# One quadrant fold per four attention slots, values five slots behind, K loaded further ahead, in a grouped-query attention block on one core

## The chip, the core and the metric

The kernel runs on one NeuronCore of a Trainium2 chip. Its engines work side by side and wait for each other through semaphores: TensorE (PE; matmuls, into PSUM), its weight loads (PEld), VectorE (DVE), ScalarE (ACT), GpSimd (POOL), and SyncE (SP), which here issues nearly all DMA transfers. The metric is the device time of one execution in microseconds (us), lower is better; single executions of one kernel lie 0.4 us apart in the three of the kernel before.

A profile is one execution. Its first 23 us (loads, first projections) vary. So besides the times this document uses a length read from the start times in the trace: **from the first scores matmul to the last matmul of all** (start to start). It is called the *stretch*; it is 321.51 us in the kernel before.

## The reference

Two independent problems, A and B, of the same form; outputs side by side.

```python
B, Sq, D = 16, 32, 1024;  Hq, Hkv, Sk, Dh = 32, 4, 512, 128
q = (x @ wq).reshape(B, Sq, Hq, Dh).transpose(0, 2, 1, 3)
k, v = repeat(k_cache, 8, axis=1), repeat(v_cache, 8, axis=1)
p = softmax(einsum("bhqd,bhkd->bhqk", q, k) * Dh ** -0.5)
out = einsum("bhqk,bhkd->bhqd", p, v).transpose(0, 2, 1, 3).reshape(B, Sq, Hq * Dh) @ wo
```

All bf16. One (batch, kv head) pair has 8 query heads x 32 queries = 256 columns against 512 keys. There are 2 x 64 = 128 such pairs.

## The kernel before

The kernel goes through 128 *slots*, one pair each, plus a few to drain. In slot i it issues the scores of pair i (keys on partitions), their exp without a row maximum, the row sums on VectorE, and the values product of an earlier pair. Around these it weaves *units*: single matmuls of the query and output projections, so that PE always has work. K and V come in *groups* of four slots, 512 KB each; K is transposed by the DMA. A *fold* is a small PE matmul: it adds the row sums, which VectorE leaves in four partition quadrants, over the quadrants. In the code and the profile s_ps are scores, p_sb their exps, cs the row sums before the fold, kT and v_sb groups of K and V, wo_sb 1 MB blocks of the output weights.

```python
def partial_sums(i):                       # DVE: 32x32 block transpose + sum -> per quadrant
    j, q = divmod(i, 2)
    if q == 0: parts[j] = work.tile([P, 2, KC, REP], FP32, name="parts")
    nc.vector.tensor_reduce(out=parts[j][:, q, :, :]..., in_=st[i]["p"]..., axis=AX.X,
                            op=ALU.add, apply_transpose=True)
def chunk_sums(j): ...                     # DVE: sum over the 4 key chunks -> cs
def fold_sums(j):                          # PE: adds the 4 partition quadrants, spreads the result
    sums = pair[j] = psum.tile([P, 2 * REP], FP32, name="sums", tag="sums", bufs=1)
    nc.tensor.matmul(sums[:], lhsT=fold[:]..., rhs=cs[:]..., start=True, stop=True)
def reciprocals(j):                        # DVE: 1/sum, then spread over the queries
    nc.vector.reciprocal(out=rall[:, j, :], in_=pair.pop(j)[:])
    r = rcp[j] = work.tile([P, 2 * REP, SQ], FP32, name="r")
    nc.vector.transpose(...)

# [...] plan of loads: the sync engine gets them in the order of their slots
for j in range(2, 2 * NG // GRP):          # GRP = 4, NG = 64
    at(GRP * (j - 1), load_k, j)
    at(GRP * (j - 1) + 2, load_v, j)
# [...]
        at(NG - 12 + nh * 8 + hg * 2, load_wo, 0, nh, hg)   # output weights of A, 8 x 1 MB

for i in range(total_slots + 3):
    live = i < total_slots
    j, odd = divmod(i, 2)
    if live: do_loads(i); scores(i)        # 4 matmuls of 256 columns
    run(units, 1)                          # 1 matmul of 512 columns
    if not odd and 1 <= j <= NG: chunk_sums(j - 1)
    if i >= 3: values(i - 3)               # 4 matmuls of 256 columns
    if odd and 1 <= j <= NG: reciprocals(j - 1)
    if not odd and j >= 2: normalize(j - 2)
    run(units, 5)
    if not odd and 1 <= j <= NG: fold_sums(j - 1)
    if live: partial_sums(i)
    run(units, 1 - (i % 4 == 3))
```

## Time and profile before

350.65 us, median of three runs (350.25 to 350.69). The busy times of the profiled execution (engine, busy us, share of the span):

```profile
span 349.1 us, 5460 instructions
PE 340.7 (98%) x2163; PEld 221.0 (63%) x2204; DVE 283.4 (81%) x421; ACT 179.6 (51%) x196; POOL 8.9 (3%) x21
PE 94%; DMA 3%; issue 1%; DVE 1%; ACT 0%; SPq 0%
```

The last line is the chain that ended last, by engine: PE bounds the kernel. A busy share of 98% alone would not say how full PE is, because matmuls overlap. The start times do. Consecutive 512-column matmuls start 216 ns apart and 256-column ones 109 ns apart. This is the warm spacing N/2.4 + 2.5 ns that the Trainium skill gives ("TensorE: Matmul & The Clock Gate", section "Back-to-back issue gap"), and the trace agrees. So each slot can be checked: take the time from its scores to the next slot's, and subtract its matmuls at that spacing. What is left is its *gap*:

| slots of the kernel before | gap each | sum in the stretch |
|---|---|---|
| without a fold | 0.00 us | 0.0 us |
| with a fold (63 in the loop) | 0.042 to 0.044 us | 2.71 us |
| extra in slots 80 and 118 | 0.33 and 0.12 us | 0.45 us |

These are the groups of instructions that the change touches (line, engine, operation, output<-input, shapes, count | busy us, mean ns of one | idle time of the engine before it, and the releaser):

```profile
L390 DVE TRANSPOSE_TENSOR_REDUCE parts<-p_sb 128x32 f32<-128x1024 bf16 x128 | 158.2, 1236 | 21.5 <-ACT p_sb L379 20.9
L407 PE MATMUL sums<-cs,fold 128*128 128x16 f32 x64 | 22.9, 357 | 0.1
L399 DVE TENSOR_REDUCE cs<-parts 128x16 fp32r<-128x64 f32 x64 | 16.9, 264 | 2.2
L407 PEld LDWEIGHTS sums<-cs,fold 128*128 128x128 f32 x64 | 12.1, 190 | 8.3 <-DVE cs L399 0.9
L416 DVE RECIPROCAL rall<-sums 128x16 f32<-128x16 f32 x64 | 14.1, 220 | 0.0
```

The fold's row says 357 ns. That is its time from start to end, most of it behind the matmul ahead of it. What it takes from PE is the 43 ns gap. One such slot in the timeline of PE (start us, length us):

```profile
154.43 1.24 PE L312 MATMUL q_ps<-xT,wq_sb 128*128 128x512 bf16 x5
155.32 0.36 PE L407 MATMUL sums<-cs,fold 128*128 128x16 f32 x1
155.54 0.39 PE L312 MATMUL q_ps<-xT,wq_sb 128*128 128x512 bf16 x1
155.77 0.60 PE L371 MATMUL s_ps<-qT,kT 128*128 128x256 bf16 x4
```

The fifth projection matmul of the first line starts at 155.29 and the next one, across the fold, at 155.54: 0.25 us instead of 0.216.

The sync engine's queue around the change from problem A to B, where loads are densest (start us, time the issue took us):

```profile
152.75 9.52 SPq L288 DMA_TRANSPOSE kT<-in_B_k_cache_dram  x1
162.31 0.58 SPq L267 DMA_DIRECT2D wo_sb<-in_A_wo_dram  x1
162.99 0.53 SPq L294 DMA_DIRECT2D v_sb<-in_B_v_cache_dram  x1
163.61 0.45 SPq L267 DMA_DIRECT2D wo_sb<-in_A_wo_dram  x1
164.16 8.96 SPq L288 DMA_TRANSPOSE kT<-in_B_k_cache_dram  x1
```

One group's worth of loads (K, V, two output-weight blocks) takes 11.4 us from K to K in these lines (10.9 us on average from the V load shown to the second one after it), one group of slots on PE 9.4 us. The V load in these lines is that of group 16, the first of problem B. It is issued at 163.0, landed at 170.4, and is first used at 180.0: 9.7 us to spare.

### The profile page before, as it was taken

The page shows a single profiled execution, that of the slowest core. Times are in us where ns is not written, and L with a number is a line of the kernel's source. Part 1 is how long each engine was busy: PE and PEld are TensorE (multiplying, and loading weights), DVE is VectorE, ACT ScalarE, POOL GpSimd, SP SyncE. Part 2 cuts the span into 40 slices and gives each one's busy share as a digit, 9 for nine tenths or more (in the row PEclk, how much of TensorE's full clock was granted, in tenths as well). Part 3 has the DMA queues.
Part 4 walks back from the last instruction along what each step waited for, and adds up shares of the span by engine and source line. Part 5 has one row for each costly group of instructions (what it writes and reads, how often), then busy time and mean ns, then how long its engine had stood idle before and what let it go on. Part 6 is the DMA issues. An engine that isn't in the chain of part 4 may idle for free.

```text
span 349.1 us, 5460 instructions
## 1 busy us (share of the span) xinstructions
PE 340.7 (98%) x2163; PEld 221.0 (63%) x2204; DVE 283.4 (81%) x421; ACT 179.6 (51%) x196; POOL 8.9 (3%) x21
## 2 busy tenths in 40 slices
PE   8999999999999999999999999999999999999995
PEld 4556666666666666666666666666666666666554
DVE  2218888988988898898889999999989999899710
ACT  2247667666666666666654454454454445445000
POOL 0000000000000000000000000000000000000010
PEclk9999999999999999999999999999999999999999
DMA  7999999999996999999999659996579975400000
GB/s 242 275 251 339 181 274 264 254 269 249 270 214 176 199 233 233 296 275 210 305 313 192 175 126 289 348 199 122 135 258 287 284 182 97 116 17 0 15 32 20
DMA packets 125085, 71.70 MB, mean 205 GB/s; under 512 B 73632, under 2 KB 124064, under 8 KB 125056
## 3 DMA queue, kind: packets, MB, share of 16 engines
q1 hardware_dynamic: 122848, 68.24, 81.1%
q0 software_dynamic: 720, 1.97, 1.6%
q10 hardware_dynamic: 1488, 1.11, 1.1%
q8 instruction: 18, 0.29, 0.4%
q14 instruction: 11, 0.09, 0.1%
HBM read 51.38 MB, written 2.10 MB: 153 GB/s over the span
## 4 chain that ended last, share of the span: by engine, by line
PE 94%; DMA 3%; issue 1%; DVE 1%; ACT 0%; SPq 0%
PE f_ps L331 31%; PE q_ps L312 30%; PE ob L431 16%; PE s_ps L371 16%; DMA wq_sb<-in_A_wq_dram 2%; DMA x_sb<-in_A_x_dram 1%; DVE parts L390 0%; PE sums L407 0%; DVE o_sb L343 0%; ACT o_sb L341 0%; DVE cs L399 0%; PE ok_ps L614 0%; SPq L651 0%
## 5 line engine op out<-in xcount | busy, mean ns | idle before, releaser
L379 ACT ACTIVATE p_sb<-s_ps,shift 128x1024 bf16<-128x1024 f32 x128 | 142.5, 1114 | 113.1 <-PE s_ps L371 100.4
L390 DVE TRANSPOSE_TENSOR_REDUCE parts<-p_sb 128x32 f32<-128x1024 bf16 x128 | 158.2, 1236 | 21.5 <-ACT p_sb L379 20.9
L331 PE MATMUL f_ps<-wo_sb,oT 128*128 128x512 bf16 (+1 forms) x524 | 127.9, 367 | 0.4
L312 PE MATMUL q_ps<-xT,wq_sb 128*128 128x512 bf16 x475 | 124.8, 380 | 0.6
L371 PE MATMUL s_ps<-qT,kT 128*128 128x256 bf16 x512 | 76.8, 273 | 0.9
L431 PE MATMUL ob<-p_sb,v_sb 128*128 128x256 bf16 x512 | 76.8, 273 | 0.6
L331 PEld LDWEIGHTS <-oT 128*128 128x128 bf16 x544 | 53.0, 98 | 33.8
L312 PEld LDWEIGHTS <-wq_sb 128*128 128x128 bf16 x496 | 48.3, 98 | 35.1 <-DMA wq_sb<-in_A_wq_dram 0.6
L371 PEld LDWEIGHTS <-kT 128*128 128x128 bf16 x512 | 56.9, 113 | 20.9
L431 PEld LDWEIGHTS <-v_sb 128*128 128x128 bf16 x512 | 50.1, 98 | 19.8 <-DVE oT L453 0.3
L453 DVE TENSOR_TENSOR oT<-r,ob 128x512 bf16<-128x512 f32 x64 | 43.9, 685 | 12.7 <-PE ob L431 9.3
L320 ACT CAST qT<-q_ps 128x512 bf16<-128x512 f32 x62 | 36.1, 583 | 23.7 <-PE q_ps L312 20.8
L418 DVE STREAM_TRANSPOSE r<-rall 128x512 f32<-128x512 f32 x64 | 45.5, 711 | 2.2
L407 PE MATMUL sums<-cs,fold 128*128 128x16 f32 x64 | 22.9, 357 | 0.1
L343 DVE CAST o_sb<-f_ps 128x512 bf16<-128x512 f32 (+1 forms) x16 | 10.8, 673 | 10.8 <-PE f_ps L331 10.0
L399 DVE TENSOR_REDUCE cs<-parts 128x16 fp32r<-128x64 f32 x64 | 16.9, 264 | 2.2
L407 PEld LDWEIGHTS sums<-cs,fold 128*128 128x128 f32 x64 | 12.1, 190 | 8.3 <-DVE cs L399 0.9
L345 POOL DMA_DIRECT2D out_dram<-o_sb x15 | 8.2, 549 | 329.7 <-DVE o_sb L343 299.0
L416 DVE RECIPROCAL rall<-sums 128x16 f32<-128x16 f32 x64 | 14.1, 220 | 0.0
L341 ACT CAST o_sb<-f_ps 128x256 bf16<-128x256 f32 x1 | 0.4, 372 | 22.1 <-PE f_ps L331 22.1
L497 DVE COPY xT<-xT_ps 128x512 bf16<-128x512 bf16 x4 | 1.7, 424 | 5.3 <-PE xT_ps L493 5.3
L484 PE MATMUL warm_ps<-warm 128*128 128x512 bf16 x10 | 4.2, 580 | 1.3 <-DVE warm L230 1.3
(26 smaller groups left out, 22.8 us busy)
## 6 DMA issues: line engine op xcount, KB each, us to landing
v_sb<-in_A_v_cache_dram SPq DMA_DIRECT2D x16, 512.0 KB, 4.9
wq_sb<-in_B_wq_dram SPq DMA_DIRECT2D x8, 1024.0 KB, 6.5
wo_sb<-in_A_wo_dram SPq DMA_DIRECT2D x8, 1024.0 KB, 7.6
v_sb<-in_B_v_cache_dram SPq DMA_DIRECT2D x16, 512.0 KB, 4.2
wo_sb<-in_B_wo_dram SPq DMA_DIRECT2D x8, 1024.0 KB, 9.2
wq_sb<-in_A_wq_dram SPq DMA_DIRECT2D x7, 1024.0 KB, 8.0
out_dram<-o_sb POOLq DMA_DIRECT2D x15, 128.0 KB, 3.1
kT<-in_A_k_cache_dram SPq DMA_TRANSPOSE x64, 4.5
```

Of the source, the lines that this page charges most:

```text
L312: nc.tensor.matmul(ps[:], lhsT=w[:, dc, (h % 4) * DH:(h % 4 + 1) * DH], rhs=xT[pr][:, dc, :], start=(dc == 0), stop=(dc == DC - 1),)
L320: nc.scalar.copy(out=qT[pr, g][:, :, hl, :], in_=ps[:].rearrange("p (b s) -> p b s", s=SQ),)
L331: nc.tensor.matmul(ps[:, 0:width], lhsT=oT[pr, tt][:, h, :], rhs=wo_tiles[pr, nh, h // REP][:, h % REP, off:off + width], start=(h == 0), ...
L371: nc.tensor.matmul(s_ps[:, c, :], lhsT=kT[:, i % GRP, c, :], rhs=qT[pr, g][:, b, :, :].rearrange("p h s -> p (h s)"), start=True, stop=True,)
L379: nc.scalar.activation(out=p_sb[:], in_=s_ps[:], func=ACTF.Exp, bias=shift[:], scale=SCALE)
L390: nc.vector.tensor_reduce(out=parts[j][:, q, :, :].rearrange("p c h -> p (c h)"), in_=st[i]["p"][:].rearrange("p c (h s) -> p (c h) s", s=SQ),
L399: nc.vector.tensor_reduce(out=cs[:], in_=parts.pop(j)[:].rearrange("p q c h -> p q h c"), axis=AX.X, op=ALU.add,)
L407: nc.tensor.matmul(sums[:], lhsT=fold[:].rearrange("p r s -> p (r s)"), rhs=cs[:].rearrange("p q h -> p (q h)"), start=True, stop=True,)
L416: nc.vector.reciprocal(out=rall[:, j, :], in_=pair.pop(j)[:])
L418: nc.vector.transpose(out=r[:].rearrange("p n s -> p (n s)"), in_=rall[:, j, :].unsqueeze(2).to_broadcast([P, 2 * REP, SQ]),)
L431: nc.tensor.matmul(ob[j][:, q, :], lhsT=v_sb[:, i % GRP, c, :], rhs=st[i]["p"][:, c, :], start=(c == 0), stop=(c == KC - 1),)
L453: nc.vector.tensor_tensor(out=out, in0=rcp.pop(j)[:].rearrange("p (q h) s -> p q h s", h=REP), in1=ob.pop(j)[:].rearrange("p q (h s) -> p ...
```

## The change

The intent is to take half of the fold matmuls off the bounding engine. Sums of four slots are folded at once. The reciprocals of a quad then come later, so the values product runs five slots behind the scores instead of three. That takes two more p_sb buffers, paid for with the third V buffer; V is then issued only one group ahead, and K "two groups ahead".

```diff
-                v_sb = v_tiles[j] = kv.tile([P, GRP, KC, DH], BF16, name="v_sb")
+                v_sb = v_tiles[j] = kv.tile([P, GRP, KC, DH], BF16, name="v_sb", bufs=2)
-                p_sb = work.tile([P, KC, QW], BF16, name="p_sb", bufs=5)
+                p_sb = work.tile([P, KC, QW], BF16, name="p_sb", bufs=7)
             def partial_sums(i):
-                j, q = divmod(i, 2)
+                j, q = divmod(i, 4)
                 if q == 0:
-                    parts[j] = work.tile([P, 2, KC, REP], FP32, name="parts")
+                    parts[j] = work.tile([P, 4, KC, REP], FP32, name="parts", bufs=1)
[... chunk_sums, fold_sums, reciprocals: 4 slots instead of 2; the spread of the
     reciprocals becomes a function of its own, called per pair ...]
-                at(GRP * (j - 1), load_k, j)
-                at(GRP * (j - 1) + 2, load_v, j)
+                at(GRP * (j - 2) + 2, load_k, j)
+                at(GRP * j + 1, load_v, j)
-            for i in range(total_slots + 3):
+            for i in range(total_slots + 5):
-                j, odd = divmod(i, 2)
+                j, q = divmod(i, 4)
+                folds = j >= 1 and j <= total_slots // 4
[...]
-                if not odd and 1 <= j <= NG:
+                if q == 0 and folds:
                     chunk_sums(j - 1)
-                if i >= 3:
-                    values(i - 3)
-                if odd and 1 <= j <= NG:
+                if i >= 5:
+                    values(i - 5)
+                if q == 1 and folds:
                     reciprocals(j - 1)
-                if not odd and j >= 2:
-                    normalize(j - 2)
+                    spread(2 * j - 2)
+                if q == 3 and folds:
+                    spread(2 * j - 1)
+                if q % 2 == 0 and i >= 6:
+                    normalize((i - 6) // 2)
                 run(units, 5)
-                if not odd and 1 <= j <= NG:
+                if q == 0 and folds:
                     fold_sums(j - 1)
```

More of the change, by code (lines that the diff above doesn't have):

```diff
@@ L382, in scores @@
                 st[i] = {"p": p_sb}
-            parts, rcp, pair = {}, {}, {}
+            parts, rcp, quad = {}, {}, {}
             def partial_sums(i):
-                j, q = divmod(i, 2)
+                j, q = divmod(i, 4)
                 if q == 0:
-                    parts[j] = work.tile([P, 2, KC, REP], FP32, name="parts")
+                    parts[j] = work.tile([P, 4, KC, REP], FP32, name="parts", bufs=1)
                 nc.vector.tensor_reduce(
@@ L396, in chunk_sums @@
             def chunk_sums(j):
-                cs = pair[j] = work.tile([P, 2, REP], FP32R, name="cs")
+                cs = quad[j] = work.tile([P, 4, REP], FP32R, name="cs", bufs=1)
                 with nc.allow_low_precision(reason="float32r holds the float32 sum"):
@@ L404, in fold_sums @@
             def fold_sums(j):
-                cs = pair[j]
-                sums = pair[j] = psum.tile([P, 2 * REP], FP32, name="sums", tag="sums", bufs=1)
+                cs = quad[j]
+                sums = quad[j] = psum.tile([P, 4 * REP], FP32, name="sums", tag="sums", bufs=1)
                 nc.tensor.matmul(
@@ L415, in reciprocals, with spread @@
             def reciprocals(j):
-                nc.vector.reciprocal(out=rall[:, j, :], in_=pair.pop(j)[:])
+                nc.vector.reciprocal(
+                    out=rall[:, 2 * j:2 * j + 2, :].rearrange("p j n -> p (j n)"),
+                    in_=quad.pop(j)[:],
+                )
+            def spread(j):
                 r = rcp[j] = work.tile([P, 2 * REP, SQ], FP32, name="r")
```

## The prediction

> **What bounds the kernel now.** TensorE. The page gives PE 98% busy, and the chain of waits that ended last is 94% PE. The start times in the trace say it harder: a 512-column matmul starts 216 ns after its predecessor, a 256-column one 109 ns. That is the warm spacing N/2.4 + 2.5 ns of the Trainium skill, "TensorE: Matmul & The Clock Gate", section "Back-to-back issue gap", and this trace agrees (215.8 and 109.2 by the formula). Measured from one slot's scores to the next, every slot is its matmuls at that spacing (7 or 6 projection units, 4 scores, 4 values) plus a remainder: 0.0 us in slots without a fold, 0.043 us in slots with one. Only two slots out of 128 show more, 0.33 and 0.12 us, both in the second half, where output casts (0.69 us) crowd VectorE. All the rest of PE is work that the change leaves alone. VectorE (283 us busy), ScalarE (180 us) and the DMA queue hide behind it.
>
> **What the change does.**
> - Removes 32 of 64 fold matmuls from PE. A fold costs 0.0435 us of PE time, not the 0.36 us that its row in the groups table shows, since most of that is waiting behind the previous matmul. The 32 left are 32 columns wide instead of 16; by the single-matmul latency (398+N)/2.4 of the same page (an estimate) that adds 0.007 us each. Saved: 64 x 0.0435 - 32 x 0.050 = 1.2 us.
> - VectorE: 32 fewer chunk sums (0.264 us) and reciprocals (0.220 us), the rest slightly longer: 12 to 14 us less busy time. All of it is off the path; it can only remove the two small waits, 0.2 to 0.45 us.
> - Values five slots behind: exps and sums have long been done in most slots, since PE waits for p_sb nowhere today. Worth 0. The tail gets two more slots without scores, but the same matmuls; the final check still has 22 projection matmuls (4.7 us) to hide about 3.8 us of VectorE work.
> - Loads: V now has two buffers, so it can be issued only after the values of two groups back, about 5 slots (11.8 us) before use; today the lead is about 9 slots. K's lead falls from about 8.7 to 7.5 slots: the plan is earlier, but the buffer release decides. Landing takes 4 to 9.5 us for V and up to 11.6 us for K, so both normally fit. Tightest is the stretch 150 to 195 us, where the queue carries K, V and two 1 MB output-weight blocks per group in 10.9 us against 9.4 us of PE time. Replaying those landings in the new order I get V of group 16 about 1 us before its use. I expect no wait, or one or two V waits of 1 to 3 us in all; weighted, +0.3 us.
>
> **Sum.** 350.65 - 1.2 - 0.3 + 0.3 = 349.4 us; 80% range 348.3 to 351.3. Faster by over 2%: 1%; within 2%: 97%; slower by over 2%: 2%.
>
> **What would show it.** Right: 32 sums matmuls; the remainder of fold slots 0.045 to 0.055 us, other slots 0.0; VectorE busy near 270 us; no weight load of v_sb or kT waiting for DMA; PE still 98%. Wrong on loads: PE waiting on V's DMA at 170 to 200 us. Wrong on the fold: fold slots with a remainder of 0.1 us or more.
>
> **What would make it wrong.** A 32-column fold that costs in proportion to its columns (no gain); V landing late at the change of problem (up to +4 us); the last output tiles waiting for the last normalization, which now comes right before them (up to +1 us).

## The result, and the profile after

350.86 us (350.44 to 351.17, four runs), against 350.54 us for the kernel before. The ratio is 1.0009, 95% interval 0.9992 to 1.0027: the same. (By the 2% rule every run below is "the same" too; what tells them apart are the intervals and the traces.) Ratios here are the mean time of one kernel's fast runs over the mean of the other's of the same rounds, so they are not quite the ratios of the medians quoted. Timed once more on another occasion, the unedited changed kernel gave 1.0015 (1.0001 to 1.0030).

Busy times, the chain by engine, the touched groups, and two lines of the waits (engine, line, waited for: us in total, times, longest us) of the changed kernel:

```profile
span 349.4 us, 5405 instructions
PE 341.6 (98%) x2172; PEld 217.1 (62%) x2172; DVE 274.4 (79%) x357; ACT 179.8 (51%) x196; POOL 9.0 (3%) x21
PE 93%; DMA 5%; DVE 1%; SPq 0%; issue 0%; ACT 0%
...
L399 DVE TENSOR_REDUCE cs<-parts 128x32 fp32r<-128x128 f32 x32 | 12.0, 376 | 1.1
L407 PE MATMUL sums<-cs,fold 128*128 128x32 f32 x32 | 11.4, 357 | 0.2 <-DVE cs L399 0.2
L416 DVE RECIPROCAL rall<-sums 128x32 f32<-128x32 f32 x32 | 10.3, 321 | 0.0
...
PEld L436 <- DMA v_sb<-in_B_v_cache_dram: 1.8, 1, 1.8
PEld sums L407 <- DVE cs L399: 1.5, 4, 0.7
```

PE's busy time even rose, since fewer of its records are missing in this trace (2172 of them against 2163, with 32 fewer matmuls in the program). That is why busy time is no judge here. The gaps are. There are 32 folds, as intended, and there is a wait that was not there before: weight loads from a V tile, once, 1.8 us. In the timeline, PE lines only:

```profile
182.54 0.60 PE L371 MATMUL s_ps<-qT,kT 128*128 128x256 bf16 x4
182.98 0.38 PE L331 MATMUL f_ps<-wo_sb,oT 128*128 128x512 bf16 x1
...
184.78 0.61 PE L436 MATMUL ob<-p_sb,v_sb 128*128 128x256 bf16 x4 [1.42 <-DMA v_sb<-in_B_v_cache_dram]
185.22 1.46 PE L331 MATMUL f_ps<-wo_sb,oT 128*128 128x512 bf16 x6
```

The values product should have started at 183.2 (182.98 + 0.216). It starts at 184.8, in slot 69, where the values of group 16 begin. The sync engine's queue of the changed kernel, in the same place as shown of before:

```profile
162.04 1.20 SPq L267 DMA_DIRECT2D wo_sb<-in_A_wo_dram  x2
163.34 1.96 SPq L294 DMA_DIRECT2D v_sb<-in_A_v_cache_dram  x1
165.34 7.54 SPq L288 DMA_TRANSPOSE kT<-in_B_k_cache_dram  x1
172.99 1.15 SPq L267 DMA_DIRECT2D wo_sb<-in_A_wo_dram  x2
174.23 1.62 SPq L294 DMA_DIRECT2D v_sb<-in_B_v_cache_dram  x1
```

The V load of group 16 is now issued at 174.2 instead of 163.0, behind a K transpose and two 1 MB weight blocks. By the landing times in the trace it is complete at 184.73, 10.5 us after its issue, and PE goes on at 184.78.

The whole account of the stretch, from the gaps:

| | before | after | difference |
|---|---|---|---|
| folds (63 and 31 in the loop, 0.043 us each) | 2.71 | 1.33 | -1.38 |
| fold waiting for VectorE (slots 80, 118; after: 4, 80) | 0.45 | 0.57 | +0.13 |
| V of group 16 late (slot 69) | 0 | 1.60 | +1.60 |
| rest (draining slots) | | | +0.03 |
| **first scores to last matmul** | **321.51** | **321.89** | **+0.38** |

So the expected gain came in full, and a late load took it back. This is arithmetic on two traces; the experiments test it.

### The profile page after: what moved, and what is told of

The parts are those of the page before. It is cut to its first block, busy times and chain, and to the rows that moved or that the text cites. A ratio compares the mean times of both kernels' runs of the same rounds, so it can differ in the third digit from the quotient of the medians.

```text
span 349.4 us, 5405 instructions
## 1 busy us (share of the span) xinstructions
PE 341.6 (98%) x2172; PEld 217.1 (62%) x2172; DVE 274.4 (79%) x357; ACT 179.8 (51%) x196; POOL 9.0 (3%) x21
## 4 chain that ended last, share of the span: by engine, by line
PE 93%; DMA 5%; DVE 1%; SPq 0%; issue 0%; ACT 0%
PE q_ps L312 31%; PE f_ps L331 30%; PE ob L436 16%; PE s_ps L371 15%; DMA v_sb<-in_B_v_cache_dram 3%; DMA x_sb<-in_A_x_dram 2%; PE q_ps L512 1%; DVE parts L390 0%; PE xT_ps L498 0%; PE sums L407 0%; DVE o_sb L343 0%; SPq L477 0%; SPq L474 0%; DVE cs L399 0%; ACT o_sb L341 0%
## 5 line engine op out<-in xcount | busy, mean ns | idle before, releaser
L331 PE MATMUL f_ps<-wo_sb,oT 128*128 128x512 bf16 (+1 forms) x544 | 132.8, 367 | 0.0
L312 PE MATMUL q_ps<-xT,wq_sb 128*128 128x512 bf16 x496 | 128.9, 379 | 0.0
L423 DVE STREAM_TRANSPOSE r<-rall 128x512 f32<-128x512 f32 x64 | 44.2, 691 | 1.1
L343 DVE CAST o_sb<-f_ps 128x512 bf16<-128x512 f32 (+1 forms) x16 | 10.8, 674 | 10.4 <-PE f_ps L331 10.1
L399 DVE TENSOR_REDUCE cs<-parts 128x32 fp32r<-128x128 f32 x32 | 12.0, 376 | 1.1
L407 PE MATMUL sums<-cs,fold 128*128 128x32 f32 x32 | 11.4, 357 | 0.2 <-DVE cs L399 0.2
L416 DVE RECIPROCAL rall<-sums 128x32 f32<-128x32 f32 x32 | 10.3, 321 | 0.0
L407 PEld LDWEIGHTS sums<-cs,fold 128*128 128x128 f32 x32 | 6.1, 190 | 4.8 <-DVE cs L399 1.5
L503 ACT COPY xT<-xT_ps 128x512 bf16<-128x512 bf16 x4 | 2.1, 589 | 5.9 <-DVE xT L502 5.9
```

Source lines behind the costliest of these rows:

```text
L312: nc.tensor.matmul(ps[:], lhsT=w[:, dc, (h % 4) * DH:(h % 4 + 1) * DH], rhs=xT[pr][:, dc, :], start=(dc == 0), stop=(dc == DC - 1),)
L331: nc.tensor.matmul(ps[:, 0:width], lhsT=oT[pr, tt][:, h, :], rhs=wo_tiles[pr, nh, h // REP][:, h % REP, off:off + width], start=(h == 0), ...
L343: nc.vector.tensor_copy(out=o_sb[:, 0:width], in_=ps[:, 0:width])
L399: nc.vector.tensor_reduce(out=cs[:], in_=parts.pop(j)[:].rearrange("p q c h -> p q h c"), axis=AX.X, op=ALU.add,)
L407: nc.tensor.matmul(sums[:], lhsT=fold[:].rearrange("p r s -> p (r s)"), rhs=cs[:].rearrange("p q h -> p (q h)"), start=True, stop=True,)
L423: nc.vector.transpose(out=r[:].rearrange("p n s -> p (n s)"), in_=rall[:, j, :].unsqueeze(2).to_broadcast([P, 2 * REP, SQ]),)
```

## The experiments

The two theories. **A:** the fold saves 1.4 us, and V's late arrival costs 1.6. **B:** the fold saves nothing that counts; the five-slot schedule or its tail eats it.

### Three V buffers

```diff
 (against the changed kernel)
-  name="v_sb", bufs=2)       +  name="v_sb")                  # three
-  name="p_sb", bufs=7)       +  name="p_sb", bufs=6)
-  FP32, name="r")            +  FP32, name="r", bufs=1)
-  at(GRP * j + 1, load_v, j) +  at(GRP * (j - 1) + 1, load_v, j)
```

> The changed kernel with three V buffers instead of two and V issued four slots earlier in the plan (room from six instead of seven p_sb and one instead of two r, which no engine should have to wait for). Theory A (the fold saved 32 x 0.0435 = 1.4 us, and V of group 16 landing late, because its buffer is released late, cost 1.6 us): the 1.6 us gap in slot 69 is gone, no weight load of v_sb waits for DMA, time 1.1 to 1.6 us under the changed kernel, ratio to the kernel before 0.9955 to 0.9975. Theory B (the fold saves nothing that counts; the schedule five slots behind or its tail eats it): the time stays within 0.3 us of the changed kernel, or a gap of the same size opens elsewhere, ratio 0.999 or more.

Measured: 349.82 us, ratio to the kernel before 0.9971 (0.9959 to 0.9984), correct. The stretch is 320.30 us, 1.6 under the changed kernel's 321.89. By the medians of separate rounds it is 1.0 us under the changed kernel, a little less than expected. No v_sb wait is left; V of group 16 landed 10.4 us before its use. No new gap opened, so six p_sb and one r are enough. The gaps in slots 4 (0.14 us) and 80 (0.44 us) stayed. Theory B falls: with the load out of the way, the five-slot kernel is faster by what its folds save.

### The loads alone

```diff
 (against the kernel before)
-  name="v_sb")                        +  name="v_sb", bufs=2)
-  at(GRP * (j - 1), load_k, j)        +  at(GRP * (j - 2) + 2, load_k, j)
-  at(GRP * (j - 1) + 2, load_v, j)    +  at(GRP * j - 1, load_v, j)
```

> The kernel before with only the loads of the change: two V buffers, K one place earlier in the plan, V issued when its buffer comes free (about 5 slots before use). Theory A: a V wait of 1 to 2 us on PE at slot 67 (first values of group 16), time 1 to 2 us over the kernel before, ratio 1.003 to 1.006; fold slots keep their remainder of 0.043 us. Theory B: no such wait without the five-slot schedule, ratio 0.999 to 1.001.

Measured: 350.73 us, ratio 0.9994 (0.9981 to 1.0007), stretch 321.51 us, exactly that of the kernel before. The expected wait did not come: V of group 16 had 3.1 us to spare, V of group 17 only 0.7. A had missed something here. The V buffers and the lead of five slots are as in the changed kernel, but with values three slots behind, V's place in the plan is two slots earlier (63 instead of 65), while the output weights keep theirs. Six of their eight blocks are ahead of V of group 16, not seven. If that one block is the difference, putting the weights two slots earlier must bring the wait:

```diff
 (against the kernel with the loads alone)
-  at(NG - 12 + nh * 8 + hg * 2, load_wo, 0, nh, hg)
+  at(NG - 14 + nh * 8 + hg * 2, load_wo, 0, nh, hg)
```

> The kernel before with only the loads of the change, which cost nothing in the earlier run, and now the first output weights two slots earlier in the plan, so that as many of them stand before V of group 16 as in the changed kernel. If V's late buffer and one more 1 MB block before it make the wait together: a V wait of 1 to 2.2 us on PE at slot 67, first scores to last matmul 322.5 to 323.7 us (without: 321.5), fold slots unchanged at 0.043 us. If the five-slot schedule itself makes the wait: no wait, 321.5 us.

Measured: 351.69 us, ratio 1.0030 (1.0018 to 1.0043). The stretch is 322.96 us, 1.45 longer; a gap of 1.44 us sits in slot 67. The waits of this run have it:

```profile
PEld L431 <- DMA v_sb<-in_B_v_cache_dram: 1.7, 1, 1.7
```

The added block acts by holding up the queue: V of group 16 was issued at 173.4 us instead of 169.4, and landed 7.7 us after its issue instead of 7.1. So it takes both: a V issued late, and one more block of weights before it. Neither the five-slot schedule nor the quad fold is needed for the wait.

### The other half of the cause: the weights moved

```diff
 (against the changed kernel; two V buffers kept)
-  at(NG - 12 + nh * 8 + hg * 2, load_wo, 0, nh, hg)
+  at(NG - 12 + nh * 20 + hg * (2 + nh), load_wo, 0, nh, hg)
```

> The changed kernel, two V buffers kept, but the second half of the first output weights (four 1 MB blocks) moved from slots 60 to 66 to slots 72 to 81, so that they no longer stand in the queue before V of group 16. Theory A with the queue as the second half of the cause: the gap in slot 69 vanishes as in the run with three buffers, ratio 0.9955 to 0.9975, and no new gap at slots 84 to 88 where these weights are first used. If the two buffers alone make V late, whatever stands before it: the gap stays at 1 us or more.

Measured: 349.36 us (349.07 to 350.49), ratio 0.9957 (0.9944 to 0.9969). The gap in slot 69 is gone: V of group 16 landed 4.1 us after its issue and 7.1 us before its use. The stretch is 320.49 us. The profiled execution is also the slowest of this kernel, because its first 23 us took 0.7 us longer than usual; such is the noise of the head. A new gap of 0.19 us appeared in slot 93, again a wait for V; it was not among the slots named.

### The fold, measured by doubling

```diff
 (against the changed kernel, in fold_sums)
-  nc.tensor.matmul(sums[:], lhsT=fold[:]..., rhs=cs[:]..., start=True, stop=True)
+  for _ in range(2):
+      nc.tensor.matmul(sums[:], lhsT=fold[:]..., rhs=cs[:]..., start=True, stop=True)
```

> The changed kernel with each of the 32 fold matmuls done twice (same result). It measures a 32-column fold by itself. Theory A (0.0435 us of PE time each): +1.4 us over the changed kernel, fold slots with a remainder of 0.08 to 0.09 us. If a fold cost the 0.36 us of its row in the groups table: +11 us. If it were hidden behind other waits: 0.

Measured: 353.98 us, ratio 1.0079 (1.0066 to 1.0092). The stretch is 324.69 us, 2.80 over the changed kernel: twice what A said. The fold slots have a gap of 0.155 us instead of 0.043. The second fold costs 0.112 us, the first 0.043. In the timeline of PE:

```profile
154.93 1.24 PE L312 MATMUL q_ps<-xT,wq_sb 128*128 128x512 bf16 x5
155.82 0.48 PE L408 MATMUL sums<-cs,fold 128*128 128x32 f32 x2
156.15 0.39 PE L312 MATMUL q_ps<-xT,wq_sb 128*128 128x512 bf16 x1
```

A fold loads float32 weights, 190 ns by its row against 98 ns for a bf16 load. Behind a 512-column matmul most of that fits into the 216 ns before the next start; behind another small fold there is nothing to hide it. That is my reading of the two numbers, not a test of it. The doubled folds add 32 x 0.112 = 3.6 us, but only 2.8 arrive, because the V wait shrank from 1.60 to 0.81 us: PE came to slot 69 2.3 us later, V landed only 1.5 us later, and a PE that comes later waits less. The same exchange should work the other way, which no run tests by itself: time saved ahead of a late load is given back at the load.

### K at its old place

```diff
 (against the changed kernel)
-  at(GRP * (j - 2) + 2, load_k, j)
+  at(GRP * (j - 1), load_k, j)
```

> The changed kernel with K put back to its old place in the plan, one group ahead instead of a little under two. If the sync engine goes through its list in order and waits only for free buffers, this place fixes only what stands before what, and between the K and V loads that order does not change: time within 0.3 us of the changed kernel, from first scores to last matmul 321.5 to 322.3 us (changed kernel 321.9), the V wait at slot 69 between 1 and 2.2 us. Rival (loading K two groups ahead is what lets the five-slot schedule run): a K wait on PE, time 2 us or more over the changed kernel.

Measured: 350.19 us, ratio 0.9994 (0.9980 to 1.0009); the stretch is 320.65 us, the V wait only 0.35 us. The rival fell: PE never waited for K, whose smallest reserve was 1.0 us (0.7 in the repeat below). But the expected wait of 1 us or more was a miss too, and the stretch lies below the stated range. It was repeated beside the changed kernel in the same rounds:

> The changed kernel once more, unedited, to see how much its V wait varies from execution to execution, and to time it on the same chip as the next run. If the size of the wait depends on how the transfers happened to fall: a V wait at slot 69 again, anywhere from 0.3 to 2 us; the rest of the stretch from first scores to last matmul as before (321.9 less its wait of 1.6, so 320.3, plus the wait). If 1.6 us is fixed: 1.5 to 1.7 us again.

> The kernel with K at its old place once more. The first profile of it showed a V wait of 0.35 us instead of the 1 us or more that was expected. If that was the draw of one execution: time within 0.3 us of the changed kernel in the same rounds. If the old place of K really shortens the wait: 0.5 us or more under the changed kernel.

Measured: the changed kernel again 350.98 us, ratio 1.0015 (1.0001 to 1.0030), V wait 1.69 us, inside the "1.5 to 1.7 us again", stretch 321.99. K at its old place again 350.00 us, ratio 0.9971 (0.9958 to 0.9984), V wait 0.62 us, stretch 320.92. The intervals do not overlap: the "K two groups ahead" line makes this kernel about 1 us *slower*. What it does is seen in the queue. With K at its old place:

```profile
166.52 0.76 SPq L267 DMA_DIRECT2D wo_sb<-in_A_wo_dram  x1
167.34 8.05 SPq L288 DMA_TRANSPOSE kT<-in_B_k_cache_dram  x1
175.44 0.57 SPq L267 DMA_DIRECT2D wo_sb<-in_A_wo_dram  x1
176.11 0.53 SPq L294 DMA_DIRECT2D v_sb<-in_B_v_cache_dram  x1
```

Between the last K and V of group 16 there is one weight block instead of two. The plan's slots are not times. The sync engine works through its list in order. It is held up by long issues (7.54 and 8.05 us for the K transposes in the lines shown of the two kernels), and it stops where a buffer is not free. Where such a wait takes place, the Trainium skill says of DMAs issued by GpSimd ("DMA: Bandwidth & Descriptors", section "Anatomy of one DMA — SWDGE (gpsimd) path"): "any semaphore wait happens on the issuing sequencer before dispatch". The trace agrees for the sync engine; in the changed kernel SP's own largest wait is this one:

```profile
SPq L294 <- PE ob L436: 71.7, 20, 8.9
```

It is V waiting for the values to free its buffer, with everything behind it waiting too. V of group 16 is not among these 20: its buffer was free at about 172.0 us, when the values of group 14 ended, and the queue came to it only at 174.2. Moving K by two slots in the plan changes nothing in the order of K against V, only which weight blocks stand between them. From issue to landing, V of group 16 took 4.1 us with no block directly before it (weights moved), 7.1 us with one (K at its old place, both runs), and 10.5 or 10.6 us with two (changed kernel, both runs). The other traces fit: 7.1 to 7.7 us with one, 9.6 to 10.3 us with two.

### Values five slots behind, alone

```diff
 (against the kernel before)
-  for i in range(total_slots + 3):   +  for i in range(total_slots + 5):
-  if i >= 3: values(i - 3)           +  if i >= 5: values(i - 5)
-  if not odd and j >= 2:             +  if not odd and j >= 3:
-      normalize(j - 2)               +      normalize(j - 3)
-  name="p_sb", bufs=5)               +  name="p_sb", bufs=6)
-  name="outp", bufs=3                +  name="outp", bufs=1      # room
```

> The kernel before with only the values five slots behind instead of three (six p_sb; to make room for them, one output staging tile instead of three), folds by pairs, three V buffers, old loads. The prediction gave this step 0: first scores to last matmul 321.3 to 321.8 us (before: 321.5), ratio 0.9985 to 1.0015. Rival: the longer tail without scores costs 0.5 us or more, or the longer lag removes the two small gaps in slots 80 and 118 (then 321.1).

Measured: 350.76 us, ratio 1.0006 (0.9993 to 1.0019), stretch 321.56 us against 321.51. The five-slot schedule is free but for a gap of 0.05 us in slot 4, and it also buys nothing: the gaps in slots 80 and 118 are still there.

### A version that beats both

What is left in the three-buffer version besides its folds are the gaps in slots 4 and 80. The second, in the changed kernel's timeline:

```profile
210.00 0.69 DVE L343 CAST o_sb<-f_ps 128x512 bf16<-128x512 f32 x1 [1.03 <-PE f_ps L331]
210.60 1.24 DVE L390 TRANSPOSE_TENSOR_REDUCE parts<-p_sb 128x32 f32<-128x1024 bf16 x1
211.88 0.37 DVE L399 TENSOR_REDUCE cs<-parts 128x32 fp32r<-128x128 f32 x1
212.30 0.28 PE L407 MATMUL sums<-cs,fold 128*128 128x32 f32 x1 [0.17 <-DVE cs L399]
```

An output cast delays the last row sums of the quad, the chunk sums follow, and PE, in order, stands at the fold. In the kernel before, where that cast began at 209.98, the fold started at 212.17; the wider chunk sum (0.37 us instead of 0.26) is what makes the difference. The remedy is to ask for the fold later:

```diff
 (against the three-buffer version)
   run(units, 1)
   if q == 0 and folds:
       chunk_sums(j - 1)
+  if q == 1 and folds:
+      fold_sums(j - 1)
[...]
   run(units, 5)
-  if q == 0 and folds:
-      fold_sums(j - 1)
```

> Three V buffers as in the earlier run, and the fold matmul moved from the end of slot 4j to after the scores of slot 4j+1, 0.9 us later, so that it need not wait for VectorE behind an output cast. If the two gaps left in that run (0.14 us in slot 4, 0.44 us in slot 80) are such waits, both vanish: first scores to last matmul 319.7 us (that run: 320.3; before: 321.5), ratio to the kernel before 0.993 to 0.9965. Rival: the later reciprocals hold up the normalizations, and gaps appear before the values; then 320.3 or more.

Measured: 348.52 us (348.52 to 349.00), ratio 0.9948 (0.9935 to 0.9961), correct; the kernel before had 350.42 in these rounds. The stretch is 319.73 us, 319.7 was expected. Both gaps are gone; the largest left besides the folds' is 0.02 us. VectorE now sits idle for 3.4 us in all before the reciprocals, which costs nothing:

```profile
L416 DVE RECIPROCAL rall<-sums 128x32 f32<-128x32 f32 x32 | 11.2, 350 | 3.4 <-PE sums L407 0.2
L407 PE MATMUL sums<-cs,fold 128*128 128x32 f32 x32 | 11.7, 367 | 0.0
PE 98%; DVE 0%; ACT 0%; issue 0%; DVEq 0%
```

The last line is the chain by engine: DMA is out of it.

## Why the prediction was right or wrong

The measured 350.86 us is inside the stated range and the class "same" was right, but the class says little, since the doubled folds are "same" too. The point, 349.4, was 1.5 us too low: the gain that it forecast did not show in the time.

- **PE bounds, at the plain matmul spacing, with 0.043 us per fold: right.** Apart from the doubled folds, every trace of the experiments has 0.042 to 0.044 us in its fold slots (0.05 to 0.06 in one slot of some), and nothing in the others but the waits named above.
- **Fold saving, predicted 1.2 us: it was 1.38.** The 32-column fold was to cost 0.050 us, with an estimate from the skill's single-matmul formula, which the page gives for the latency of one bf16 matmul and not for a spacing. It costs the same 0.043 as the 16-column one. The doubling run showed that its cost is not a fixed price either: 0.112 us without a long matmul ahead.
- **VectorE "12 to 14 us less busy", "near 270": too much.** It was 9.0 us (283.4 to 274.4), since a chunk sum of twice the size took 376 ns instead of 264, a reciprocal 321 instead of 220. And the gain from it, -0.3 us in the sum, was of the wrong sign: +0.13 us. The small wait in slot 118 did go, with the fold of that slot. But the longer chunk sum stands directly before the fold: the wait in slot 80 grew from 0.33 to 0.44 us, and one of 0.13 us is new in slot 4.
- **Values five slots behind, worth 0: right,** shown alone (321.56 against 321.51).
- **The loads: mechanism right, size wrong.** The prediction named group 16 of V, the stretch of 150 to 195 us, and a wait of 1 to 3 us; the wait is 1.6 to 1.7 us, in both traces of the changed kernel. But it put V's arrival about 1 us before its use, and so entered the wait with "+0.3". V came 1.6 us after. This term was mis-sized by 1.3 us, and it is most of the error. Which end of it slipped stays open. The traces offer one candidate: PE itself comes earlier. Slot 69 began at 182.54 us instead of 183.99 in the kernel before, because two more slots at the start carry no values product (0.44 us each) and 17 folds fewer came before it. A replay with the old slot times would have PE ask for V 1.45 us too late.
- **"K: the plan is earlier, but the buffer release decides": half right.** It decides when K can be issued. But the place in the plan also decides which weight blocks come between K and V, and that was worth about 1 us (two pairs of traces, and times 350.98 against 350.00).
- **The last normalization before the last output tiles, feared at up to 1 us: did not happen** (+0.03 us in the drain).

What stays open: why V lands 1 us or more earlier with K between the weight blocks, although by the plan seven blocks are ahead of it in both orders. One thing in the traces fits in size, and no run tests it: in both traces of the changed kernel the sync engine stood still for 1.3 to 1.4 us before V of group 14, until its buffer was free. With K at its old place it was still busy with earlier issues when that buffer came free, and the stop was 0.1 us. The traces show the latencies, not what happens inside the DMA engines.

## What to carry to other kernels

When an engine is full to the last gap, account for every slot of it as known spacing plus a remainder; then a saving of 0.04 us per instruction and a single late load of 1.6 us are both visible, where busy shares and the total time show nothing. Before a buffer is given up to pay for a saving elsewhere, look for the densest stretch of its queue and ask which large transfer will stand directly before it there: the plan of an in-order queue is an order, not a schedule. An instruction's price depends on its neighbours, so price a removal by the gap around it, not by its row in the profile.

## What the Trainium skill lacked or had wrong

- "TensorE: Matmul & The Clock Gate", section "Back-to-back issue gap": it calls N/2.4 + 2.5 ns only the isolated gap and gives about 131 ns per 512-column matmul as the sustained figure for streams of weight load and matmul. In this stream of that kind the spacing is 216 ns (and 109 ns for 256 columns): the "isolated" formula holds, as it does in the page's own account of a matmul's phases.
- The same page, section "LDWEIGHTS": P / 1.2 is 107 ns for 128 columns. Here 98 ns in bf16 but 190 ns in float32, for which the section has no figure of its own (a later one only leaves float32 out of its fast weight loads), and a second float32 fold directly behind the first cost PE 112 ns instead of 43.
- "DMA: Bandwidth & Descriptors" does not say how long issuing a DMA transpose holds the sync engine. For 512 KB of K of problem B it was 1.8 to 4.5 us where only a V load stood between it and the K before, and up to 10.1 us with weight blocks among them. It also gives no latency behind queued transfers: V of group 16 took 4.1 us, 7.1 to 7.7 us and 9.6 to 10.6 us behind zero, one and two 1 MB blocks that followed a K transpose. All V loads of problem B in these traces spread more: 3.7 to 5.3, 3.8 to 8.0 and 5.4 to 10.6 us.
